# Another order and other engines for the small operations of a fused attention and two-layer kernel

## Chip, cores and metric

The kernel runs on one core of a Trainium2 chip. The metric is the device time of one execution in microseconds, as the median of several runs. All data starts in DRAM and the result ends there.

## What is computed

Chunked attention feeds two dense layers. The inputs q, k and v are 4 x 8 x 768 x 64 (batch, heads, sequence, head size), so there are 3072 tokens of 512 numbers.

```python
# attention: for every chunk of 32 queries, keys are 8 memory keys and the context from 16 left to 8 right
a = exp(s - max(s)); a = a / (sum(a) + 1e-9); out = a @ v_full
x = out.transpose(0, 2, 1, 3).reshape(3072, 512)
# first layer, w_in 512 x 1024, w_out 1024 x 512
h = x @ w_in
solu = h * softmax(h)
x = ((solu - mean(solu)) / sqrt(var(solu) + 1e-6) * g_ln) @ w_out
# second layer, w_in 512 x 2048, w_out 2048 x 512
h = x @ w_in
y = (h * clip(h + 3, 0, 6) / 6) @ w_out
```

The weights arrive as 64-bit floats and are turned into 32-bit ones on the chip.

## The kernel before, in words

**Tiles and precision.** Tokens are cut into 24 tiles of 128 (numbered 0 to 23). Every product with weights is done as three matmuls of type fp32r: each operand is split into a high part (on ACT, L337 and L895) and a low part, the difference (on VectorE or POOL, L341 and L898), and high x high, high x low and low x high are added up in PSUM.

**Weights.** A block of 128 x 512 is converted in steps: abs (L304 on ACT, L306 on VectorE), hold, a clamp (L311), three bit operations on VectorE (L315, L318, L321), then split or store. Names w1 and wo are those of the first layer, w2 those of the second. The 32 blocks of w2 are loaded, converted and written back to DRAM during the loop, two in a step; sum_pair (L848, L850 on POOL, four instructions) forms sums of blocks, and sums_out writes them, as the second layer uses a scheme of 7 products for blocks of 2 x 2.

**The order is written by hand.** Each engine runs its instructions in program order. The program is a list of names, expanded by a dispatcher; where an entry ends in a letter, P, D or A is the engine (POOL, VectorE, ACT). FIRST holds the fill, tiles 0 to 6 and, in entries that begin with @, step 7 of the loop. BODY is run for steps 8 to 23. LAST leads from the first layer to the second, a generator (unchanged) does the middle, CHANGE leads from the second layer's first product to its second, and a generated end (unchanged) closes.

**A step m of the loop** does, for tile m, m1 (x @ w_in in two halves of 12 matmuls, L694) and the ln_ entries: max (L703), exp (L709), den (L715), solu (L720), mean, sq, var, pow (L738 on POOL) and norm (L743). For a group of earlier tiles it does parts of m2 (@ w_out, L798), whose result m2_e copies out of PSUM as x2o (L808). For tile m - 1 it transposes solu (ln_p, L547 or L750) and splits it (ln_h L337, ln_l L341). For tiles ahead it runs attention: v_p (m + 1, L668), x_h and x_l (split of x, m + 1), s_max, s_sub, s_exp, s_sum and s_norm (softmax, m + 2; s_norm writes pn, L642), p_q (transposes of pn, m + 2, L583) with p_e (copies, L298), s_p (scores, m + 3, L540), and qk_p (transposes of q and k, m + 4, L547) with q_e and k_e (copies into kT, L298 on ACT, L300 on VectorE). qk uses the same PSUM buffer as m1's result h, so it waits until solu has read h, and the next m1 waits until q_e and k_e have read qk. k_e has four pieces: 0 is 128 x 448 and 1 is 128 x 256, pieces 2 and 3 are 128 x 96. DMAs are issued by SP, in program order too.

**The second layer.** mm(n) is one unit of 42 matmuls of 128 x 256 (L1006) into one of two sets of PSUM banks; o1 to o4 on VectorE (L1027, L1030, L1034, L1038) add up its products, then come relu (ACT, L1041) and clip (VectorE, L1044). Its operands are made by w_hi, w_lo, x_sum (POOL, L967), x_hi and x_lo. In the last stage, g4(i) is 21 matmuls (L1093) on operands from g_sum (L1072), g_hi and g_lo; g4:0 and g4:1 belong to one output tile, g4:2 to the next.

The conversion of w2 is tied to the step by these lines; a step handles block 2(m - 7) and block 2(m - 7) + 3:

```python
        def w2_of(m, x):
            u = 2 * (m - STEADY) + 3 * x
            return u if u < 2 * NF2 else None
```

Of the kernel before, what the change touches and what calls it, by code (L numbers as in the profile page):

```python
# [35 lines left out]
    w1_hi:0,P spread_mem_v:0,0,A s_rec:1 warm:4 v_p:0 s_norm:1,P p_p:1 k_e:3,1,A k_e:3,0,A w1_bits:4,1 s_max:2
    q_e:3,0,A q_e:3,1,A w1_bits:4,2 w1_hi:4,P load_k:4 s_sub:2 s_exp:2 w1_bits:5,2 load_q:4 x_h:0,0 s_p:3 s_sum:2
    k_p:4,0 x_l:0,0 p_e:1,1,A w1_hi:5,P warm:1 q_p:4 k_e:4,0,A w1_lo:4,D q_e:4,0,A p_e:1,0,A load_w1:2 w1_lo:5,D
    s_rec:2 load_v:1 s_max:3 w1_lo:0,P w1_abs:2,A load_q:5 spread_mem_v:1,0,A m1:0,0,0 load_w1:7 k_p:4,1
    spread_mem_v:1,64,A k_e:4,1,A s_norm:2,P w1_hold:2,D q_e:4,1,A w1_bits:2,0 w1_bits:2,1 m1:0,1,0 s_sub:3 s_exp:3  # L40
    v_p:1 load_w1:6 w1_bits:2,2 s_p:4 x_h:1,0 s_sum:3 x_l:1,0 load_k:5 w1_abs:7,A load_v:2 p_p:2 q_p:5 q_e:5,0,A
    s_rec:3 s_norm:3,D p_e:2,0,A w1_hi:2,P load_q:6 w1_lo:2,P w1_hold:7,D w1_abs:6,A w1_bits:7,0 w1_bits:7,1
    p_e:2,1,A q_e:5,1,A early_open m1:1,0,0 w1_bits:7,2 load_v:3 m1:1,1,0 w1_hold:6,D w1_bits:6,0 w1_bits:6,1
    w1_bits:6,2 w1_hi:7,A w1_lo:7,D m1:0,0,1 k_p:5,0 k_e:5,0,A load_k:6 w1_hi:6,A w1_lo:6,D load_wo:5 k_p:5,1 v_p:2
    k_e:5,1,A p_p:3 p_e:3,1,A load_wo:1 s_max:4 s_sub:4 p_e:3,0,A m1:0,1,1 ln_max:0 s_exp:4 m1:1,0,1 x_h:2,0 x_l:2,0
    k_p:6,1 s_p:5 ln_exp:0 s_sum:4 q_p:6 load_wo:0 m1:1,1,1 ln_den:0 k_p:6,0 q_e:6,1,A wo_abs:5,D wo_abs:1,A
    ln_solu:0 ln_mean:0 ln_sq:0 k_e:6,1,D ln_var:0 s_rec:4 wo_hold:5,D ln_max:1 s_norm:4,P load_wo:6 v_p:3 q_e:6,0,A
    m1:2,1,0 s_edge:5 s_max:5 s_sub:5 ln_exp:1 m1:2,1,1 m1:2,0,0 consts wo_abs:0,A ln_pow:0 load_wo:2 s_exp:5
    load_wo:7 k_mem:6,D k_e:6,0,A ln_den:1 p_p:4 x_h:3,1 wo_hold:1,P wo_bits:5,0 ln_norm:0 wo_bits:5,1 p_e:4,1,A
    s_sum:5 load_v:4 wo_bits:1,0 wo_hold:0,D ln_solu:1 wo_bits:5,2 x_l:3,1 ln_p:0,0 ln_h:0,0,1 m1:2,0,1 ln_p:0,1  # L50
    load_q:7 ln_mean:1 s_rec:5 ln_sq:1 ln_max:2 m1:3,1,0 ln_var:1 wo_bits:0,0 m1:3,1,1 load_wo:4 p_e:4,0,A load_k:7
    wo_bits:1,1 wo_abs:7,A wo_abs:6,A wo_bits:0,1 s_norm:5,D wo_hold:6,D wo_bits:0,2 s_p:6 ln_exp:2 wo_abs:4,D
    wo_bits:6,0 ln_den:2 ln_l:0,0,1 v_p:4 m1:3,0,0 load_g wo_hi:0 load_wo:3 ln_pow:1 x_h:4,1 wo_abs:2,D ln_h:0,1,1
    ln_solu:2 m1:3,0,1 ln_mean:2 ln_sq:2 x_l:4,1 wo_hold:4,D ln_norm:1 ln_p:1,0 ln_h:1,0,1 load_q:8 s_edge:6
    ln_max:3 s_max:6 wo_bits:6,1 wo_bits:1,2 s_sub:6 ln_p:1,1 ln_var:2 ln_pow:2 m1:4,1,0 p_p:5 ln_l:1,0,1 ln_exp:3
    p_e:5,1,A s_exp:6 wo_bits:4,0 q_p:7 ln_norm:2 p_e:5,0,A m1:4,1,1 m1:4,0,0 load_v:5 ln_l:0,1,1 q_e:7,1,A s_sum:6
    m1:4,0,1 wo_bits:6,2 q_e:7,0,A ln_p:2,0 ln_den:3 s_rec:6 wo_lo:0 wo_bits:4,1 k_p:7,0 ln_max:4 wo_hold:2,P
    k_e:7,0,D ln_h:1,1,1 ln_l:1,1,1 load_k:8 k_p:7,1 k_e:7,1,D early_close v_p:5 wo_abs:3,A ln_solu:3 ln_h:2,0,1
    ln_l:2,0,1 ln_p:2,1 ln_exp:4 ln_den:4 ln_solu:4 s_p:7 wo_hold:7,D k_p:8,0 x_h:5,1 s_norm:6,P p_p:6 wo_bits:2,0
    ln_h:2,1,1 p_e:6,0,A wo_bits:7,0 x_l:5,1 ln_l:2,1,1 k_e:8,0,A wo_hi:1 m1:5,1 p_e:6,1,D wo_bits:4,2 wo_hi:4  # L60
    k_p:8,1 load_v:6 wo_bits:2,1 v_p:6 wo_bits:2,2 ln_mean:4 ln_sq:4 wo_bits:7,1 ln_mean:3 wo_hold:3,P wo_lo:1
    wo_hi:2 q_p:8 wo_hi:5 wo_bits:3,0 wo_bits:3,1 m1:5,0 ln_sq:3 wo_lo:4 m2:0,0 wo_bits:3,2 wo_hi:3 wo_lo:2 wo_lo:5
    ln_var:3 load_v:8 wo_lo:3 m2:0,1 wo_hi:6 k_e:8,1,D wo_bits:7,2 x_h:6,1 s_max:7 ln_pow:3 wo_hi:7 x_l:6,1 m2:0,3
    load_w2:1 ln_norm:3 ln_max:5 ln_p:3,1 wo_lo:7 w2_abs:1,A wo_lo:6 ln_p:3,0 m2:0,4 m2:0,5 ln_exp:5 q_e:8,0,A
    ln_h:3,0,1 s_sub:7 q_e:8,1,A s_exp:7 ln_den:5 m2:0,2 ln_solu:5 ln_mean:5 m1:6,0 ln_l:3,0,1 m2_e:0,1 ln_sq:5
    ln_var:5 s_sum:7 s_rec:7 load_w2:0 w2_abs:0,A m2_e:0,0 m1:6,1 ln_var:4 ln_pow:5 ln_norm:5 ln_pow:4 w2_hold:1,D
    ln_h:3,1,0 s_norm:7,D p_p:7 w2_bits:1,0 load_k:9 ln_norm:4 load_v:7 ln_l:3,1,0 m2:0,6 ln_p:4,1 m2_s:0,0
    p_e:7,1,A ln_max:6 p_e:7,0,A ln_h:4,1,0 s_p:8 w2_bits:1,1 w2_bits:1,2 v_p:7 x_h:7,0 load_w2:3 load_k:10
    w2_store:1 ln_p:4,0 ln_l:4,1,0 ln_p:5,0 k_mem:9,D m2:0,7 w2_hold:0,D ln_exp:6 ln_den:6 ln_solu:6 ln_mean:6
    s_max:8 ln_sq:6 m2:0,8 ln_var:6 x_l:7,0 m2:0,9 m2:0,10 load_q:9 s_sub:8 s_exp:8 m2_e:0,2 ln_h:4,0,0 s_sum:8  # L70
    s_rec:8 s_norm:8,P ln_l:4,0,0 m2_s:0,1 m2:0,11 load_q:10 ln_h:5,0,0 q_p:9 load_v:9 q_go:9,A ln_l:5,0,0 m2_s:0,2
    block_p:9 ln_p:5,1 ln_h:5,1,0 load_k:11 block_e:9,A m2_e:0,3 w2_abs:3,A ln_pow:6 ln_norm:6 @m2:0 block_p:10
    block_e:10,A load_k:12 ln_l:5,1,0 late_turn p_p:8 w2_hold:3,P @qk_p_at:6 @k_e_at:6,3 @s_p_at:6 @k_e_at:6,0
    @s_max load_k:13 @q_e_at:6 @k_e_at:6,1 @k_e_at:6,2 load_q:11 @m2:2 m2_s:0,3 @s_sub @s_exp @w2_bits:0,0
    @w2_bits:0,1 @w2_bits:0,2 load_q:12 @w2_bits:1,0 @w2_bits:1,1 p_e:8,1,A p_e:8,0,A @w2_bits:1,2 @load_w2:0
    @w2_store:1 @sum_pair @sums_out @s_sum @s_norm @load_w2:1 @m1:0 @m1:1 @ln:max @w2_abs:0 @ln_p @ln:exp @ln:den
    @s_p @ln:solu @v_p @x_h @ln:mean @m2:3 @m2:1 @ln_h:0 @ln_l:0 @m2_e @qk_p @p_p @load_q @ln_h:1 @ln_l:1 @k_e:0
    @k_e:3 @x_l @q_e @k_e:1 @k_e:2 @load_k @k_mem @ln:sq @ln:var @w2_hold:0 @ln:pow @w2_abs:1 @p_e:1 @w2_hold:1
    @ln:norm @w2_store:0 @p_e:0 @m2_s @load_v
# [1410 lines left out]
```

## Time and profile before

| what | value |
|---|---|
| median of 3 runs | 869.97 us |
| lowest, highest | 866.45, 871.79 us |
| profiled execution | 870.14 us |
| its span | 868.3 us |
| TensorE matmul busy | 847.9 us, 98% of the span |
| VectorE (DVE) busy | 739.5 us, 85% |
| ScalarE (ACT) busy | 476.6 us, 55% |
| GpSimd (POOL) busy | 256.3 us, 30% |

PE is TensorE's matmul unit, DVE VectorE, ACT ScalarE, POOL GpSimd, SP the engine that issues DMAs. Times of the trace are counted from the start of the span; 1.84 us of the execution lie outside it. A busy time is an average over stages with different limits, so the windows of a stage are read beside it, and "idle before" an instruction, with the instruction that ended it, tells what an engine waited for.

### The profile page before, as it was taken

The numbers are of one execution on the slowest core, as the hardware profiler recorded it, in microseconds if no ns is written. First come the engines' busy times: TensorE is split into PE (matmuls) and PEld (weight loads), VectorE is DVE, ScalarE is ACT, GpSimd is POOL, SyncE is SP. The second block draws the span as 40 slices with busy tenths as digits, with TensorE's granted clock in tenths as the row PEclk, the third lists the DMA queues.
The fourth block names the chain that finished last, engine by engine and source line by source line (L and its number), as shares of the span: only waits on it lengthen the run. The fifth ranks groups of instructions, "written<-read, shape, count | busy, mean of one in ns | idle before, by whom it ended". The sixth has DMA issues, their size and how long they took to land.

```text
span 868.3 us, 21875 instructions
## 1 busy us (share of the span) xinstructions
PE 847.9 (98%) x8526; PEld 803.2 (92%) x8526; DVE 739.5 (85%) x1510; ACT 476.6 (55%) x946; POOL 256.3 (30%) x226
## 2 busy tenths in 40 slices
...
DVE  6899977787878779574999989889999999999995
...
GB/s 234 214 262 70 116 157 198 234 204 236 212 235 197 228 176 168 149 111 193 209 180 160 243 134 206 174 167 229 239 270 258 165 137 147 149 137 143 136 134 62
DMA packets 181552, 157.88 MB, mean 182 GB/s; under 512 B 105160, under 2 KB 155848, under 8 KB 181448
## 3 DMA queue, kind: packets, MB, share of 16 engines
...
q8 instruction: 67, 1.10, 0.5%
...
## 4 chain that ended last, share of the span: by engine, by line
PE 80%; DVE 11%; DMA 2%; issue 2%; ACT 2%; POOL 1%; DVEq 0%; POOLq 0%; ACTq 0%; SPq 0%
PE acc L1093 26%; PE acc L1006 21%; PE m L798 13%; PE h L694 10%; PE tp L668 2%; PE s L540 1%; DVE f_s L1044 1%; PE qk L547 1%; PE idle L1161 1%; PE tp L547 1%; DVE so L720 1%; PE sc L595 1%; DMA woraw<-in_moe_w_out_dram 1%; DVE lst L703 1%; PE tp L583 1%
## 5 line engine op out<-in xcount | busy, mean ns | idle before, releaser
L798 PE MATMUL m<-lnh,wo 128*128 128x256 f32 (+1 forms) x704 | 143.3, 295 | 3.7 <-DVE x2o L808 2.8
L798 PEld LDWEIGHTS m<-lnh,wo 128*128 128x128 f32 x704 | 113.9, 189 | 6.6 <-DVE x2o L808 3.1
L1041 ACT ACTIVATE f_s<-f_e,constants 128x512 f32<-128x512 f32 x96 | 67.9, 720 | 83.3 <-DVE f_e L1034 69.7
L694 PE MATMUL h<-w,xh 128*128 128x512 f32 x336 | 105.9, 396 | 1.1 <-ACT kT L298 1.1
L798 PE MATMUL m<-lnl,wo 128*128 128x256 f32 (+1 forms) x352 | 102.0, 290 | 0.0
L694 PEld LDWEIGHTS h<-w,xh 128*128 128x128 f32 x336 | 61.3, 188 | 13.0 <-ACT kT L298 1.3
L1044 DVE SCALAR_TENSOR_TENSOR f_s<-f_s,f_e 128x512 f32<-128x512 f32 x96 | 72.0, 758 | 0.7 <-ACT f_s L1041 0.7
L798 PEld LDWEIGHTS m<-lnl,wo 128*128 128x128 f32 x352 | 66.7, 189 | 0.6
L311 POOL TENSOR_SCALAR w2t<-w2t 128x512 f32<-128x512 f32 x30 | 59.8, 1992 | 20.8 <-ACT w2t L304 20.8
L694 PE MATMUL h<-w,xl 128*128 128x512 f32 x168 | 65.6, 390 | 0.0
L808 DVE COPY x2o<-m 128x512 f32<-128x512 f32 (+1 forms) x26 | 16.6, 646 | 40.8 <-PE m L798 39.6
L709 ACT ACTIVATE e<-h,lst 128x1024 f32<-128x1024 f32 x24 | 26.8, 1115 | 29.9 <-DVE lst L703 29.9
L895 ACT ACTIVATE b_qb<-f_kn 128x384 fp32r<-128x384 f32 (+1 forms) x48 | 27.7, 576 | 27.9 <-DVE f_kn L1072 15.4
L1030 DVE TENSOR_TENSOR f_e<-acc,f_e 128x512 f32<-128x512 f32 x48 | 32.9, 685 | 8.0 <-PE acc L1006 7.1
L694 PEld LDWEIGHTS h<-w,xl 128*128 128x128 f32 x168 | 31.5, 188 | 6.9
L642 POOL TENSOR_TENSOR pn<-pe,ast 128x512 f32<-128x512 f32 x21 | 22.3, 1063 | 50.5 <-DVE ast L638 40.3
L627 ACT ACTIVATE pe<-pe 128x512 f32<-128x512 f32 x24 | 15.2, 632 | 39.6 <-DVE pe L622 38.2
L703 DVE TENSOR_REDUCE lst<-h 128x1 f32<-128x1024 f32 x24 | 29.2, 1217 | 6.1 <-PE h L694 6.0
L1038 DVE TENSOR_TENSOR f_e<-acc,f_e 128x512 f32<-128x512 f32 x48 | 33.0, 687 | 1.1 <-PE acc L1006 0.2
L720 DVE SCALAR_TENSOR_TENSOR so<-h,lst,e 128x1024 f32<-128x1024 f32 x24 | 30.8, 1283 | 0.9
L341 DVE TENSOR_TENSOR lnl<-tp,lnh 128x512 fp32r<-128x512 f32 x41 | 28.1, 684 | 3.6 <-ACT lnh L337 3.6
L848 POOL TENSOR_TENSOR sums<-w2t,sums 128x256 f32<-128x256 f32 x24 | 20.8, 865 | 33.5 <-DVE w2t L321 33.5
...
## 6 DMA issues: line engine op xcount, KB each, us to landing
...
```

The costliest lines, as they stand in the source:

```text
L311: ENG[eng].tensor_scalar(out=tf, in0=tf, scalar1=U_LO, scalar2=U_HI, op0=ALU.max, op1=ALU.min)
L341: (POOL if far else DVE).tensor_tensor(lo, r, hi.bitcast(F32), ALU.subtract)
L694: PE.matmul(h[:, f], a[:, kt], w[kt][:, f * 512:(f + 1) * 512], start=n == 0, stop=n == 3 * NKT - 1)
L703: DVE.tensor_reduce(st_t[i][:, 2:3], h_t[i].rearrange("p a b -> p (a b)"), axis=AX.X, op=ALU.max, negate=True)
L720: DVE.scalar_tensor_tensor(out=so_t[i], in0=h_t.pop(i).rearrange("p a b -> p (a b)"), scalar=st[:, 5:6], in1=e_t[i], op0=ALU.mult, op1=ALU ...
L798: PE.matmul(acc, w[fc // 2][:, fc % 2, dc * P:(dc + 1) * P], a[:, fc], start=fresh and k == 0, stop=k == len(todo) - 1, skip_group_check=True)
L1006: PE.matmul(o, w[wl][:, c * P:(c + 1) * P], x[xl][:, c], start=m == 0 and half == 0, stop=m == 5, skip_group_check=True)
L1030: DVE.tensor_tensor(c_of(n)[1], bank(n % 2, 2), wide(c_of(n)[0][:, 1]), ALU.add)
L1038: DVE.tensor_tensor(c, bank(n % 2, 3), c, ALU.add)
L1041: ACT.activation(out=g_of(n)[k], in_=c_of(n)[k], func=AF.Relu, bias=three, scale=1.0)
L1044: DVE.scalar_tensor_tensor(out=g_of(n)[k], in0=g_of(n)[k], scalar=6.0, in1=c_of(n)[k], op0=ALU.min, op1=ALU.mult)
L1093: PE.matmul(bank(t % 2, k)[:, half], g[al][:, G_BLOCK[p]], b_op[j, p][bl], start=j == 0 and m == 0 and half == 0, stop=j == NU - 1 and m = ...
```

## The change

The set of operations is the same but for one form (ln_norm on ACT, two instructions, for tiles 4, 5 and step 7). What changes is the order of all four lists and the engine of some entries:

- w2: a step m handles block 2(m - 8) and block 2(m - 8) + 3, one step later than before; step 7 only converts block 1, and step 23 is the last with a block. sum_pair and sums_out follow.
- Engines in BODY: s_norm from POOL to VectorE, k_e 1, 2 and 3 from ACT to VectorE, w2_abs:0 from ACT to VectorE. Elsewhere: some conversions, copies and s_norm of the first list swapped between the three engines; the two block_e to VectorE.
- BODY's order, below in full. On TensorE only ln_p changes place, from behind qk_p to ahead of it. TURN, run in the last step, moves to near the start of the step.
- FIRST is rewritten as a whole.
- LAST: mm:0 moves from behind m2:10,7 to between m2:10,2 and m2:10,3; m2_e:9,1 comes ahead of m2_e:10,0.
- CHANGE: the order g4:0, g4:2, g4:1 becomes g4:0, g4:1, g4:2; the entries around them are shifted.

```diff
 BODY = """
-    m1:1 m1:0 w2_bits:0,0 m2:0 s_max w2_bits:0,1 w2_bits:1,0 s_sub w2_bits:0,2 ln:max w2_bits:1,1 s_exp w2_bits:1,2
-    sum_pair m2:1 ln:exp w2_store:0 v_p ln:den ln:solu s_sum s_p load_w2:0 x_h qk_p k_e:0 ln:mean q_e w2_store:1
-    k_e:1 w2_abs:0 k_e:3 s_norm k_mem w2_hold:0 ln_p m2:2 m2:3 load_w2:1 sums_out ln:sq load_v x_l turn m2_e k_e:2
-    p_p ln:var load_k ln_h:0 ln:pow ln_l:0 ln_h:1 ln:norm w2_abs:1 p_e:1 m2_s load_q ahead w2_hold:1 ln_l:1 p_e:0
+    s_max w2_bits:0,0 s_sub w2_bits:0,1 m1:1 turn w2_bits:0,2 m1:0 m2:0 m2:1 ln:max w2_bits:1,0 v_p w2_bits:1,1
+    ln:exp ln:den ln:solu w2_bits:1,2 s_exp sum_pair load_w2:0 ahead s_sum x_h w2_store:0 s_p ln_p ln:mean load_w2:1
+    ln:sq ln:var qk_p k_e:2,D x_l k_e:0,A k_e:3,D s_norm:D q_e:A k_e:1,D k_mem m2:2 m2:3 w2_abs:0,D sums_out ln_h:0
+    ln:pow m2_e:D ln_l:0 load_k ln_norm:D ln_h:1 w2_abs:1,A load_q p_p w2_hold:0,P m2_s w2_hold:1,P p_e:1,A ln_l:1
+    p_e:0,A load_v w2_store:1
 """
...
 LAST = """
...
-    load_w:5 load_w:4 w_lo:2 x_hi:0,2 x_hi:0,6 x_lo:0,2 w_hi:4 m2:10,2 m2_e:10,0 m2_e:9,1 x_sum:0,3 load_w:6 m2:10,3
-    m2_s:10,0 x_hi:0,4 m2:10,4 m2:10,5 x_lo:0,6 w_lo:4 w_hi:6 load_w:7 x_lo:0,5 m2_s:9,1 w_lo:6,pool w_hi:5 w_lo:5
-    load_w:8 w_hi:8 m2:10,6 m2:10,7 load_w:10 w_hi:7 m2_e:10,1 x_lo:0,4 mm:0 p1:0 o1:0 w_lo:7,pool load_w:9 m2:10,9
...
+    x_hi:0,2 ln_l:23,1 x_sum:0,4 x_hi:0,6 m2:10,0 m2:10,1 x_lo:0,2 x_sum:0,3 w_hi:4 w_hi:6 x_hi:0,4 m2:10,2 w_lo:3
+    load_w:7 w_hi:5 m2_e:9,1 w_hi:7 x_lo:0,4 x_lo:0,6 w_lo:6,pool load_w:10 w_hi:10 w_lo:4 m2_e:10,0 mm:0 p1:0
+    w_lo:5 m2:10,3 load_x:1 m2:10,6 w_lo:10,pool o1:0 m2:10,4 o2:0 m2:10,5 load_w:8 m2_s:9,1 load_w:14 m2:10,7 o3:0
...
 CHANGE = """
...
-    b_lo:13,1,pool g4:0 load_b:19 g_lo:2,0 g_hi:1,1 g_load:6 o3:47 g_lo:2,1 g_lo:1,1 relu:46,0 g_hi:4,0 relu:46,1
-    g_sum:4,1 g_sum:4,2 o4:47 g_lo:4,0 relu:47,0 fetch_b:21 clip:46,0 g_sum:3,1 relu:47,1 g_sum:4,4 b_hi:19,1
-    clip:46,1 g_sum:4,3 g_hi:4,1 g_sum:3,2 clip:47,0 g_lo:4,1 clip:47,1 fetch_b:22 g_sum:6,3 b_lo:18,1,pool g_sum:3,3
-    g_sum:3,4 g_sum:6,1 g4:2 g4:1 g_hi:3,0 g_hi:5,0 g_load:8 fetch_b:14 g_lo:3,0 g_load:7 g_sum:6,2 g_hi:3,1 g_hi:6,0
...
+    o2:47 g_hi:2,1 o3:47 g4:0 g_load:4 g4:1 g_store:44 g_lo:2,0 g_lo:2,1 relu:46,0 b_lo:13,1,pool clip:46,0
+    g_sum:4,1 g_load:3 fetch_b:14 o4:47 g_sum:3,1 g_store:45 g_sum:3,3 g_sum:3,2 relu:46,1 g_sum:4,2 g_sum:3,4
+    g_sum:4,3 g_sum:4,4 g_load:6 g_hi:4,0 fetch_b:22 fetch_b:15 g_lo:4,0 relu:47,1 g_hi:4,1 b_lo:18,1,pool clip:46,1
+    load_b:19 g4:2 g_lo:4,1 relu:47,0 g4:4 clip:47,0 clip:47,1 fetch_b:16 g_load:8 g_hi:6,0 g_sum:6,1 g_hi:5,0
...
-    def ln_norm(i):
+    def ln_norm(i, eng="D"):
         st = st_t.pop(i)
         so = so_t[i]
-        DVE.tensor_scalar(out=so, in0=so, scalar1=st[:, 7:8], scalar2=st[:, 10:11], op0=ALU.add, op1=ALU.mult)
+        if eng == "A":
+            ACT.activation(out=st[:, 11:12], in_=st[:, 7:8], func=AF.Copy, scale=st[:, 10:11])
+            ACT.activation(out=so, in_=so, func=AF.Identity, bias=st[:, 11:12], scale=st[:, 10:11])
+        else:
+            DVE.tensor_scalar(out=so, in0=so, scalar1=st[:, 7:8], scalar2=st[:, 10:11], op0=ALU.add, op1=ALU.mult)
...
         def w2_of(m, x):
-            u = 2 * (m - STEADY) + 3 * x
-            return u if u < 2 * NF2 else None
+            return 2 * (m - STEADY - 1) + 3 * x
+
+        def w2_next(m, x):
+            u = w2_of(m, x) + 2
+            return 0 <= u < 2 * NF2 and u != 1
...
-        def l_s_norm(m):
+        def l_s_norm(m, eng):
             if ok(m + 2):
-                s_norm(m + 2, "P")
+                s_norm(m + 2, eng)
 
         def pair_of(m):
-            return m % 2, (m - STEADY) // 2
+            return 1 - m % 2, (m - STEADY - 1) // 2
...
-        def l_k_e(m, n):
+        def l_k_e(m, n, eng):
             if ok(m + 4):
-                qk_k(m + 5, n, "A")
+                qk_k(m + 5, n, eng)
```

The other functions that take an engine now (l_p_e, l_q_e, l_w2_abs, l_w2_hold, l_m2_e) change in the same manner.

## Rows read from the trace of the kernel before

**Rows 1.** The page, parts 1 and 2: busy times, and VectorE in 40 slices.
```profile
PE 847.9 (98%) x8526; PEld 803.2 (92%) x8526; DVE 739.5 (85%) x1510; ACT 476.6 (55%) x946; POOL 256.3 (30%) x226
...
DVE  6899977787878779574999989889999999999995
```

**Rows 2.** What TensorE waited for: us in total, times, longest us.
```profile
PE m L798 <- DVE x2o L808: 2.8, 1, 2.8
PE tp L750 <- DVE sc L605: 1.4, 1, 1.4
...
PE h L694 <- DVE so L720: 1.1, 1, 1.1
PE h L694 <- ACT kT L298: 1.1, 1, 1.1
...
PE acc L1093 <- DVE f_e L1038: 1.0, 1, 1.0
...
PE tp L583 <- POOL pn L642: 0.5, 1, 0.5
```

**Rows 3.** Windows: us, then PE, PEld, DVE, ACT, POOL busy, PEclk, DMA, GB/s.
```profile
8.20:61.20 53.00, 51.80 (x550) 41.30 (x550) 46.37 (x85) 40.77 (x82) 20.17 (x20) 1.00 0.96 243
61.20:92.50 31.30, 28.94 (x280) 23.17 (x281) 31.04 (x51) 25.98 (x53) 16.13 (x13) 1.00 0.41 92
92.50:142.70 50.20, 47.13 (x515) 42.34 (x513) 38.09 (x66) 31.50 (x70) 14.52 (x14) 1.00 0.60 159
...
187.40:202.08 14.68, 14.68 (x206) 13.35 (x205) 11.67 (x21) 8.87 (x21) 8.62 (x9) 1.00 0.85 241
...
387.20:391.20 4.00, 3.99 (x14) 3.99 (x15) 3.41 (x4) 1.98 (x4) 1.59 (x2) 0.57 0.78 244
```

**Rows 4.** Timeline of a loop step, VectorE and TensorE: start us, us, engine, instruction.
```profile
193.47 1.21 DVE L703 TENSOR_REDUCE lst<-h 128x1 f32<-128x1024 f32 x1
...
197.80 0.46 PE L547 MATMUL qk<-ident,q_raw 64*128 64x64 f32 x8
...
201.77 0.60 PE L583 MATMUL tp<-ident,pn 128*128 128x128 f32 x4
...
203.90 0.69 DVE L341 TENSOR_TENSOR lnl<-tp,lnh 128x512 fp32r<-128x512 f32 x1
```

**Rows 5.** Groups by form: xcount, busy us, mean ns, idle before, releasers.
```profile
L642 DVE TENSOR_TENSOR pn<-pe,ast 128x512 f32<-128x512 f32 x3 | 2.2, 743 | 0.1
L642 POOL TENSOR_TENSOR pn<-pe,ast 128x512 f32<-128x512 f32 x21 | 22.3, 1063 | 50.5 <-DVE ast L638 40.3 <-DVE s L603 7.3 <-PE sc L595 2.8
L298 ACT ACTIVATE kT<-qk 128x96 f32<-128x96 f32 x27 | 7.1, 263 | 0.0
L300 DVE COPY kT<-kmT 128x128 f32<-128x128 f32 x7 | 1.5, 218 | 0.2
L306 DVE TENSOR_SCALAR wot<-woraw 128x512 uint32<-128x512 uint32 x2 | 0.8, 413 | 0.0
L304 ACT ACTIVATE w2t<-w2raw 128x512 f32<-128x512 f32 x32 | 21.4, 669 | 6.7 <-DMA w2raw<-in_moe_w_in_dram 3.7 <-issue 3.0
L298 ACT ACTIVATE kT<-qk 128x256 f32<-128x256 f32 x13 | 5.0, 388 | 0.0
```

**Rows 6.** Timeline, SP's queue and ACT: one load of w2 and its first use.
```profile
314.26 0.38 SPq L429 DMA_DIRECT2D w2raw<-in_moe_w_out_dram  x1
...
322.99 0.68 ACT L304 ACTIVATE w2t<-w2raw 128x512 f32<-128x512 f32 x1 [2.99 <-issue]
```

**Rows 7.** Timeline of the transition to the second layer: POOL, VectorE and TensorE.
```profile
380.88 1.75 POOL L967 TENSOR_TENSOR f_pn<-f_v,f_pe 128x512 f32<-128x512 f32 x1
381.41 1.78 DVE L898 TENSOR_TENSOR b_wb<-f_pb,b_wb 128x512 fp32r<-128x512 f32 x1
...
384.81 0.68 DVE L898 TENSOR_TENSOR b_wb<-f_qb,b_wb 128x512 fp32r<-128x512 f32 x1
...
386.02 1.14 DVE L808 COPY x2o<-m 128x384 f32<-128x384 f32 x2
...
387.21 0.45 PE L798 MATMUL m<-lnh,wo 128*128 128x384 f32 x1 [2.80 <-DVE x2o L808]
```

More of the change, by code (lines that the diff above doesn't have):

```diff
@@ L36 @@
[L36 to L79, printed above, removed]
+    zero:km0,D zero:km1,D zero:kn0,D load_w1:1 w1_abs:1,A idle_fill:10 idle_fill:19 load_mem_k:0 load_q:0 mem_p:0
@@ new lines @@
+    ln_h:0,0,1 load_v:5 wo_abs:7,A ln_l:0,0,1 wo_bits:0,0 wo_bits:0,1 wo_bits:1,1 load_k:8 ln_max:2 wo_bits:0,2
+    s_p:6 wo_abs:4,A wo_hold:4,D ln_norm:1,D ln_exp:2 ln_den:2 wo_abs:6,D wo_bits:4,0 ln_p:0,1 x_h:4,1 wo_hi:0
+    s_edge:6 wo_bits:1,2 ln_p:1,0 ln_h:0,1,1 m1:3,1,0 m1:3,1,1 ln_solu:2 wo_hold:6,D x_l:4,1 m1:4,0,0 ln_mean:2
+    ln_sq:2 ln_var:2 q_p:7 ln_p:1,1 wo_bits:6,0 wo_bits:6,1 ln_pow:2 s_norm:5,D s_max:6 ln_h:1,0,1 ln_norm:2,D
+    s_sub:6 q_e:7,0,A q_e:7,1,A ln_l:1,0,1 p_p:5 s_exp:6 ln_max:3 ln_l:0,1,1 p_e:5,1,A m1:4,0,1 p_e:5,0,A s_sum:6
```

203 lines of the change are left out of this document (122 added, 81 removed).

## Prediction

> **What bounds the kernel now.** I read the page first: busy times, then the slices. TensorE's matmul engine is busy in 98% of the span, VectorE in 85%, and VectorE's slices reach 9 in several stretches [rows 1]. So TensorE is the bound nearly everywhere, and the order and engine of small operations can only buy back what it idles, or make it idle more. Its waits come next. The ones that matter are few and named [rows 2]: 2.8 us for x2o, the output copy of the first layer; 1.4 and 1.1 us in the front for VectorE; 1.1 us for ACT's copies to kT; 1.0 us for the third output addition, just before the last stage's products go on; 0.5 us for POOL's pn. All the waits of that view together make 14.4 us, those left out here under 1 us each but for 2.3 at the start, with 1.7 us more where the clock was down (below). That is the purse.
>
> Then the windows [rows 3]. From 8.20 to 61.20 us TensorE was busy 51.80 of 53.00 us, part of it with filler matmuls. From 61.20 to 92.50 it lost 31.30 - 28.94 = 2.36 us while VectorE was busy 31.04 of 31.30: there VectorE is the bound. From 92.50 to 142.70 it lost 50.20 - 47.13 = 3.07 us. One step of the loop lasts 14.68 us, all of them TensorE's, with VectorE at 11.67, ACT at 8.87 and POOL at 8.62 us. There the change cannot win, only lose. Last, the timeline of a step and of the transition.
>
> The profiled execution took 870.14 us (span 868.3 and 1.84 around it), 0.17 above the median shown. I subtract from 870.1.
>
> **The loop, 16 steps.** The list of operations is the same, so TensorE's 14.68 stay. Three edits load VectorE. s_norm leaves POOL, 1063 ns, for VectorE, 743 ns. Three of four k_e copies leave ACT; VectorE's nearest copies take 218 ns (128x128), and the 96-column ones 263 on ACT. The abs of one weight block costs 413 ns on VectorE against 669 on ACT [rows 5]. I take 0.74 + 2 x 0.2 + 0.4 (the 256-column copy, 388 on ACT) + 0.41 = 1.95; not all steps have all, and over the loop I count 26.7 us, or 1.67 a step. VectorE comes to 11.67 + 1.67 = 13.3 us of 14.68. It holds, with 1.3 to spare. Below, the bound is nothing gained or lost; above, the first rival.
>
> In-order queues ask for more than a sum. In the step shown, which begins at 187.40, the maximum starts at 193.47 (6.07 into it), and qk, which waits for solu's read of the shared bank, at 197.80 (10.40) [rows 4]. The new order puts five short VectorE entries (0.4 to 0.7 each, 2.7 in all at their spacing) ahead of the maximum, and the last ln_l of the step before ends 2.5 us into the step (203.90 + 0.69 - 202.08 [rows 4]). That gives 5.2 to 5.9: no later than now. solu then ends near 9.9, half a microsecond before it is needed. s_norm, behind x_l and two k_e copies, ends at 13.3 to 13.9; its transpose is due at 201.77 - 187.40 = 14.37 [rows 4]. Slack 0.4 to 1: I take 0. One wait goes: p_q:22 waited 0.5 for POOL [rows 2], where s_norm was behind the long clamps of POOL's queue; on VectorE nothing long is before it. Gain 0.55.
>
> **Weights one step later.** Three bit instructions of the first x = 0 block, about 2.0 us of VectorE, leave step 7, which lies in the loaded front, and turn up in step 23, which had none. In step 23 they are covered by 14.68 of TensorE. In the front they are part of the next term.
>
> **The front.** Ahead of the last wo_lo that the first m2 needs, VectorE's list sums to 85.7 us before and 86.1 after, pricing each entry by its form: no shorter. What can shrink is its idle time before 61 us (53.00 - 46.37 = 6.6 [rows 3]) and the order in which results fall due. ln_norm:3 and wo_lo:6 come 1.4 and 3.2 us earlier in the list, and the whole first list falls from 110.5 to 107.4. Up to 99 us TensorE waits 4.9 in all, 1.4 and 1.1 of it in rows 2. I take 1.5 back; the ends are +4.9 and, as a rearranged saturated queue may be late elsewhere, -1.5.
>
> From 99 us to the loop, 0.54 + 1.10 + 0.62 = 2.3 us are lost, the 1.1 for kT on ACT [rows 2]. The k_e copies now lie earlier or on VectorE, and step 7's VectorE list is 10.1 instead of 12.0. Late x_h and x_l of tile 8 cost about 0.8 by my count. Gain 1.4 (0 to 2.3).
>
> **LAST.** mm:0, the first product of the second layer, moves from behind m2:10,7 to between m2:10,2 and m2:10,3. Before, m2:10,3 began at 387.21 after 2.80 idle, since m2_e:9,1 had to empty its bank, and on VectorE's queue that copy (386.02, two together 1.14) stood behind two 1.78 us splits [rows 7]. After the pause the granted clock was 0.57 over 4.00 us, that is near the lower of its two levels (1.2 of 2.4 GHz), against 1.00 in the stages shown [rows 3]: 4.00 x 0.43 = 1.7 lost too. mm:0 is 42 matmuls of about 115 ns, 4.9 us. It covers the 2.8 and keeps TensorE busy, so the 1.7 goes as well, if its operands are there. x_lo:0,4 is the late one: by POOL's sums I put it at 385 to 386, and mm:0 reads it at about 387. Gain 4.5; less 1.0 for what VectorE, full in the stretch that follows, gives back (0 to 1.5, or all 4.5 if the operand is late). I take 3.5.
>
> **CHANGE.** g4:1 now follows g4:0 and goes on in the same output tile's PSUM, so the 1.0 us wait for the third addition [rows 2] is filled by 21 matmuls. VectorE is full here; I take 0.5 (0 to 1.0). The code after the last matmul isn't touched.
>
> Sum: 0.55 + 1.5 + 1.4 + 3.5 + 0.5 = 7.4. 870.1 - 7.4 = 862.7 us.
>
> **A rule that speaks against it.** A POOL addition of 1.75 us started at 380.88, and VectorE's split at 381.41 took 1.78 instead of the 0.68 of its like at 384.81 [rows 7]. The Trainium skill, "Perfetto Trace Analysis", section "Optimizing Scalar/DVE Operations", says that the two engines share a read port and that shifting work between them may not help; the trace agrees for splits, which took 2.6 times as long, and no row shows s_norm on VectorE beside POOL's pair sums. The mechanism here, from rows, is the third rival.
>
> **Rivals.**
> First, slower: w2_abs:0 on VectorE holds the whole queue until its DMA has landed. On ACT the same wait cost nothing. One block was asked for at 314.26 and converted at 322.99, after 2.99 idle [rows 6], 8.7 us later; the new order has about 8.5 us between issue and use. For it: behind the abs stand m2_e, ln_norm, both ln_l and the next maximum. Against it: of 32 blocks only 6.7 us of idle was before the conversion [rows 5]. It decides once the wait exceeds the 1.3 us to spare: 2.99 - 1.35 = 1.6 a step, 13 us if half the steps have it, 862.7 + 13.1 = 875.8; in ten steps or more it passes 878.7.
> Second, no gain where VectorE is full: the front keeps its 4.9 and the transition gives the 3.5 back, as VectorE's sum past 392 us doesn't change. What stays is 0.55 and about 0.8: 868.7.
> Third, POOL's four pair sums (0.7 to 1.0 each) now run beside s_norm. If it waits for one, it ends at 14.0 to 14.6 against 14.37: 0.25 a step, 4.0 in all, 866.7.
> Fourth, the front loses its waits wholly, because VectorE's early idle time is used: 3.4 more, and the give-back of 1.0 and the 0.8 don't come: 862.7 - 5.2 = 857.5.
>
> **How the numbers follow.** Forecast 0.45 (its own range 858 to 868), first rival 0.12, second 0.15, third 0.08, fourth 0.20. About 1% is what a measurement of this kernel tells from no change: 861.3 and 878.7. Faster is the fourth and two fifths of the forecast, 0.20 + 0.18 = 0.38. Slower is two thirds of the first, 0.08. Same is the rest, 0.54. The range 854 to 876 leaves out the dearer half of the first rival and the fastest part of the fourth, with unknown mishaps under 0.2.
>
> **What would show it.** Right: the loop's step at 14.68 with VectorE at 13 to 13.5; no wait for x2o near 387 and clock 1.00 there; under 3.5 us of waits from 61 to 99; no pn wait. Wrong: a step of 15 or more, with VectorE's rows after w2_abs late (first rival) or s_norm over 1 us long (third); mm:0 waiting for x_lo; new waits for o1 to o4 between 400 and 460.

## The result and the profile after

The changed kernel took 856.07 us (median of 4 runs, 855.08 to 857.3), the kernel before 868.49 us in the same comparison: a ratio of 0.985 with an interval of 0.982 to 0.989. It is faster by 12.4 us where 7.4 were forecast, inside the stated range of 854 to 876 and below the 858 to 868 of the forecast itself.

The page of the changed kernel, its busy times and VectorE (DVE) in slices:

```profile
PE 845.4 (99%) x8526; PEld 802.0 (94%) x8526; DVE 760.9 (89%) x1578; ACT 464.5 (54%) x893; POOL 253.2 (30%) x214
...
DVE  6999867999999999776999988998999999999995
```

Against [rows 1], VectorE has 21 us more to do and TensorE's share rises by one per cent of a shorter span. The view of TensorE's waits is nearly empty; it answers to [rows 2] (engine, tile and line, waited for; us in total, times, longest):

```profile
PE idle L1162 <- POOL ident masks.py:199: 1.3, 1, 1.3
PE m L804 <- DVE x2o L814: 0.6, 1, 0.6
PE acc L1099 <- DVE f_e L1040: 0.6, 1, 0.6
...
PE h L696 <- DVE kT L302: 0.3, 1, 0.3
```

All waits of the front that rows 2 show (sc, so, kT) are gone or down to 0.3, pn is gone, x2o fell from 2.8 to 0.6. The 0.6 for f_e at L1040 is a wait for o3; the 1.0 of before, at L1038, was one for o4. Windows of the changed kernel (columns as in [rows 3]), in this order: the front as in [rows 3], the whole part up to tile 6's m1, a loop step, and the product that was moved (mm:0).

```profile
61.20:92.50 31.30, 31.06 (x299) 25.86 (x298) 30.52 (x55) 29.41 (x60) 18.11 (x14) 1.00 0.68 155
...
0.00:99.03 99.03, 96.46 (x918) 79.92 (x919) 86.84 (x161) 75.96 (x151) 45.93 (x45) 1.00 0.80 198
...
180.46:195.14 14.68, 14.68 (x208) 13.35 (x206) 13.84 (x26) 9.17 (x19) 8.52 (x8) 1.00 0.85 232
...
376.40:381.40 5.00, 5.00 (x45) 5.00 (x44) 4.07 (x6) 1.79 (x3) 1.50 (x2) 1.00 0.50 143
```

In the front TensorE now loses 0.24 us of 31.30 (before 2.36) although VectorE is still busy 30.52 us. The step keeps its 14.68 us with VectorE at 13.84. Where mm:0 now stands the clock is 1.00.

A ledger follows from the starts of the same work in both timelines (us; the last column is what the stage gave). In the last stage the products are counted by their matmuls, 21 to a g4:

| start of | before | after | gained so far | stage |
|---|---|---|---|---|
| m1 of tile 3 | 61.19 | 60.71 | 0.5 | fill: 0.5 |
| m1 of tile 6 | 103.94 | 99.03 | 4.9 | front: 4.4 |
| m1 of tile 9 | 158.03 | 151.10 | 6.9 | to the loop: 2.0 |
| m1 of tile 23 | 361.61 | 353.81 | 7.8 | loop: 0.9 |
| mm(2) | 410.98 | 399.46 | 11.5 | transition: 3.7 |
| mm(12) | 460.78 | 447.06 | 13.7 | ten products on: 2.2 |
| 17th g4 | 672.09 | 659.80 | 12.3 | CHANGE: -1.4 |
| end of the last matmul | 862.75 | 850.47 | 12.3 | the rest: 0 |

So three questions were left: why the front, the three rows up to tile 9's m1, gave 6.9 and not 2.9, what in LAST (the transition and the ten products behind it) gave 5.9 and not 3.5, and why CHANGE cost 1.4 instead of giving 0.5.

### The profile page after: what moved, and what is told of

Its sections match the earlier page's. It is cut to its first block, busy times and chain, and to the rows that moved or that the text cites. A ratio compares the mean times of both kernels' runs of the same rounds, so it can differ in the third digit from the quotient of the medians.

```text
span 855.5 us, 21813 instructions
## 1 busy us (share of the span) xinstructions
PE 845.4 (99%) x8526; PEld 802.0 (94%) x8526; DVE 760.9 (89%) x1578; ACT 464.5 (54%) x893; POOL 253.2 (30%) x214
## 4 chain that ended last, share of the span: by engine, by line
PE 85%; DVE 7%; DMA 3%; SPq 2%; ACT 2%; issue 1%; POOL 0%; DVEq 0%; POOLq 0%; ACTq 0%
PE acc L1099 25%; PE acc L1012 23%; PE m L804 15%; PE h L696 12%; PE tp L670 2%; PE s L542 1%; PE tp L549 1%; DVE f_s L1050 1%; PE qk L549 1%; DMA woraw<-in_moe_w_out_dram 1%; SPq L399 1%; PE idle L1162 1%; PE tp L585 1%; DMA f_xo<-sums 1%; DMA w1raw<-in_moe_w_in_dram 1%
## 5 line engine op out<-in xcount | busy, mean ns | idle before, releaser
L313 POOL TENSOR_SCALAR w2t<-w2t 128x512 f32<-128x512 f32 x31 | 66.7, 2161 | 16.6 <-DVE w2t L308 15.5
L901 ACT ACTIVATE b_qb<-f_kn 128x384 fp32r<-128x384 f32 (+1 forms) x48 | 27.6, 575 | 23.2 <-DVE f_kn L1078 12.1
L740 POOL TENSOR_TENSOR lst<-lst,constants 128x1 f32<-128x1 f32 x24 | 17.3, 722 | 58.8 <-ACT lst L736 58.8
L300 ACT ACTIVATE pb<-tp 64x512 f32<-64x512 f32 x46 | 27.2, 592 | 6.1 <-PE tp L652 4.3
L904 DVE TENSOR_TENSOR b_pb<-f_kn,b_qb 128x384 fp32r<-128x384 f32 (+1 forms) x48 | 29.5, 616 | 0.0
```

The costliest lines, as they stand in the source:

```text
L313: ENG[eng].tensor_scalar(out=tf, in0=tf, scalar1=U_LO, scalar2=U_HI, op0=ALU.max, op1=ALU.min)
L904: eng.tensor_tensor(hl[1], r, hl[0].bitcast(F32), ALU.subtract)
```

## Experiments

Every kernel below is the changed one with one thing put back or moved. The kernel before was measured again beside each group of them, with medians of 868.2 to 869.7 us, so medians of different groups that lie 1.5 us apart may be the same.

**The old first list.** FIRST of before, with the entries for the x = 0 block of step 7 taken out:

```diff
 FIRST = """
-    zero:km0,D zero:km1,D zero:kn0,D load_w1:1 w1_abs:1,A idle_fill:10 idle_fill:19 load_mem_k:0 load_q:0 mem_p:0
...
+    zero:v1,P zero:kn1,D zero:km1,D zero:v0,D load_q:0 idle_fill:10 q_p:0 load_w1:1 zero:kn0,P zero:qb,P q_e:0,0,A
...
```

> The changed kernel with the first list of before in its order and on its engines, the second weights still one step later (the entries for the x = 0 block taken out of that list). Theory A, the new first list is what takes the waits from 61 to 154 us away: TensorE starts m1 of tile 9 at 156 to 158 us as before (158.0) and not at 151.1, total 861 to 863 us. Rival B, the later weights did it, since they take 2 us and more off the loaded VectorE: start at 151 to 153, total 856 to 858.

It took 863.57 us, ratio 0.992 (0.990 to 0.995), and tile 9's m1 began at 157.06. The waits are back, as the view of TensorE's waits of this kernel shows:

```profile
PE tp L755 <- DVE sc L606: 1.6, 1, 1.6
...
PE h L695 <- ACT kT L299: 1.1, 1, 1.1
PE h L695 <- DVE so L721: 0.9, 1, 0.9
PE m L803 <- DVE wo L420: 0.9, 2, 0.5
```

Theory A holds in its start of 156 to 158 us, and its total came out 0.6 above the range: the first list is worth 6.0 us up to tile 9's m1 and 7.5 by the medians. The later weights by themselves gave at most the 1.0 us between 158.03 and 157.06.

**The new order with the old engines.** In the new first list, 42 entries go back to the engine of before, such as:

```diff
-w1_abs:1,A
+w1_abs:1,D
...
-q_e:1,0,A
+q_e:1,0,D
...
-k_e:8,1,A
+k_e:8,1,D
```

> The changed kernel with its new order in the first list, but 42 of the 43 entries that changed their engine back on the engine of before. Theory A1, the order does it (VectorE is kept busy earlier and the late results fall due in time): m1 of tile 9 within 1.5 us of 151.1, total 856 to 858 us. Rival A2, the engines do it (VectorE relieved of clamps and copies in the front): m1 of tile 9 at 155 us or later, total 860 us or more.

It took 876.22 us, ratio 1.007 (1.004 to 1.009), 0.7% slower than before. By the numbers A1 is out, but A2's reason is not shown either: 8.6 of the 20 us arise before tile 0's m1 (40.25 instead of 31.62), where VectorE is busy 23.2 of 40.25 us. Later, one copy, k_e:8,1 on VectorE behind the wo conversions, costs one wait, a row of this kernel's waits of TensorE:

```profile
PE tp L754 <- DVE kT L300: 3.6, 1, 3.6
```

So a third theory, C, was put up: order and engine only work together. Two kernels tell it from A2. One puts back only the 15 entries ahead of tile 0's m1:

> The changed kernel, with only the 15 entries ahead of tile 0's m1 on the engine that they had before (zeroing, conversion of the first weights w1, a few copies and s_norm:0). Theory C, order and engine belong together: in the new order these engines make queues that wait for a DMA or for each other, as in the run with 42 entries put back; TensorE starts m1 of tile 0 at 38 to 41 us instead of 31.6 and the delay is kept, total 863 to 866 us. Rival: the early delay gives VectorE, which is full from 60 us on, time to work ahead, so most of it is won back by tile 9: total under 860 us.

It took 864.47 us, ratio 0.995 (0.993 to 0.997); tile 0's m1 began at 41.14 and tile 9's at 158.94, so 7.8 of the 9.5 us of delay were kept. Where it begins is seen in VectorE's timeline of this kernel:

```profile
12.90 0.68 DVE L300 COPY qb<-tp 64x512 f32<-64x512 f32 x1 [4.19 <-ACT w1raw L304]
13.51 0.41 DVE L315 TENSOR_SCALAR w1raw<-w1raw 128x512 uint32<-128x512 uint32 x1
```

q_e:1,0, now on VectorE, waits 4.19 us, and the first weight's bits stand behind it: 13.51, where the changed kernel has them at 8.31. TensorE then waits for ACT and VectorE in its fill:

```profile
PE sc L595 <- ACT kT L298: 2.6, 2, 2.1
PE tp L490 <- DVE kmT L300: 1.4, 1, 1.4
```

The granted clock is lower there too, as the window of 20.00 to 31.60 shows, first of this kernel, then of the changed one:

```profile
20.00:31.60 11.60, 9.61 (x63) 7.22 (x62) 6.51 (x14) 5.25 (x11) 5.02 (x7) 0.55 0.73 169
```

```profile
20.00:31.60 11.60, 11.45 (x149) 9.19 (x150) 11.20 (x22) 9.92 (x20) 5.75 (x7) 1.00 0.80 184
```

The other kernel keeps the old order and takes all new engines:

> The changed kernel with the first list in the order of before, but all its entries on the engines of after (weights one step later, as in the run with the old first list, which took 863.6 us). Rival A2, the engines by themselves relieve VectorE: total 860 us or less, fewer waits for VectorE from 61 to 99 us. Theory C, order and engine belong together: no gain against 863.6, total 863 us or more, with new waits where the old order has the entry late on the new engine.

It took 867.46 us, ratio 0.999 (0.997 to 1.000): the engines alone are worth nothing here, they cost 3.9 us against the old list, with new or longer waits of TensorE:

```profile
PE tp L756 <- DVE sc L607: 2.3, 1, 2.3
PE h L696 <- ACT kT L300: 2.2, 1, 2.2
```

Of its delay, 4.5 us arise before tile 0's m1 (35.66 instead of the old list's 31.16). So both of these totals hang much on the fill. The stretch from tile 3's m1 to tile 6's lies behind it, and there theory C can be read without the fill. "Slowed" are VectorE's instructions that took over 0.15 us more than their form's quick price (a tenth of its instructions in all fourteen traces are as quick or quicker), with what they took above it in sum:

| first list | stretch, us | VectorE busy, us | slowed |
|---|---|---|---|
| kernel before | 42.8 | 41.8 | 7, by 5.0 us |
| old order, old engines | 42.9 | 41.9 | 7, by 5.0 us |
| old order, new engines | 42.2 | 41.3 | 5, by 4.2 us |
| new order, 42 old engines | 45.1 | 40.6 | 3, by 3.2 us |
| new order, 15 old engines | 37.9 | 36.7 | 3, by 1.0 us |
| changed kernel | 38.3 | 37.0 | 3, by 1.0 us |

VectorE runs 66 or 67 instructions in each of the six, and the 45.1 has the wait of 3.6 for kT in it. Neither half of the change does it here either, and the 15 early engines have no part in this stretch. Theory C holds at both ends.

**The loop's engines and its list.**

```diff
-    ln:sq ln:var qk_p k_e:2,D x_l k_e:0,A k_e:3,D s_norm:D q_e:A k_e:1,D k_mem m2:2 m2:3 w2_abs:0,D sums_out ln_h:0
+    ln:sq ln:var qk_p k_e:2,A x_l k_e:0,A k_e:3,A s_norm:P q_e:A k_e:1,A k_mem m2:2 m2:3 w2_abs:0,A sums_out ln_h:0
```

> The changed kernel with the three loaded edits of the loop undone: s_norm on POOL, k_e 1 to 3 and w2_abs:0 on ACT, same order. Theory: the loop's step is TensorE's 14.68 us with either engine, VectorE only falls from 13.8 to about 12 us a step; total 855.5 to 857.5, with at most one wait for pn of 0.5 us or so back. Rival: the moves are what lets the step run without waits, since ACT's copies hold up the next m1; then 0.2 us a step or more come back, 859 us or more.

It took 856.36 us, ratio 0.984 (0.981 to 0.988), no different from the changed kernel. The same step of it as the changed kernel's above, by its window:

```profile
178.18:192.86 14.68, 14.68 (x208) 13.36 (x206) 12.14 (x21) 9.55 (x22) 9.90 (x9) 1.00 0.84 225
```

VectorE has 1.7 us less in it, and TensorE's 14.68 stand. No wait for pn came back, though s_norm is on POOL again. With the whole BODY of before instead:

> The changed kernel with the loop's list of before, order and engines, weights one step later. Theory: the loop is bound by TensorE in both lists, so the step stays 14.68 us; what returns is the one wait for pn (0.5) and the waits at the seam between the first list and the loop, since the lists were laid out for each other: 856.5 to 859 us. Rival: the new list of the loop carries part of the front's gain: 860 us or more, with waits in step 8.

It took 859.2 us, ratio 0.988 (0.985 to 0.992). Its longest new waits of TensorE are one at qk in step 8, the seam (146.08), and one for a norm behind the loop (369.28):

```profile
PE qk L549 <- issue: 1.2, 1, 1.2
...
PE tp L756 <- DVE so L749: 0.7, 1, 0.7
```

The theory holds for the seam, its upper end a little low, but its wait for pn did not return: s_norm was on POOL in the old order too, and the view has no row for pn. The steps between are bound by TensorE, though not alike: with the old list every other one lasts about 14.75 us, in this kernel as in the kernel before, and TensorE is busy in all of it. One such step of the kernel before:

```profile
202.13:216.88 14.75, 14.74 (x207) 13.37 (x206) 11.70 (x21) 8.86 (x21) 9.40 (x9) 1.00 0.80 208
```

With the new order nearly all steps have 14.68, on either engines. What TensorE spends the 0.07 on stays open.

**LAST.** mm:0 and its first readers go back behind m2:10,7, in the new list:

```diff
-    load_w:7 w_hi:5 m2_e:9,1 w_hi:7 x_lo:0,4 x_lo:0,6 w_lo:6,pool load_w:10 w_hi:10 w_lo:4 m2_e:10,0 mm:0 p1:0
-    w_lo:5 m2:10,3 load_x:1 m2:10,6 w_lo:10,pool o1:0 m2:10,4 o2:0 m2:10,5 load_w:8 m2_s:9,1 load_w:14 m2:10,7 o3:0
+    load_w:7 w_hi:5 m2_e:9,1 w_hi:7 x_lo:0,4 x_lo:0,6 w_lo:6,pool load_w:10 w_hi:10 w_lo:4 m2_e:10,0
+    w_lo:5 m2:10,3 load_x:1 m2:10,6 w_lo:10,pool m2:10,4 m2:10,5 load_w:8 m2_s:9,1 load_w:14 m2:10,7 mm:0 p1:0 o1:0 o2:0 o3:0
```

> The changed kernel with mm:0 and what reads it (p1:0, o1:0, o2:0) back behind m2:10,7; the rest of the new list for the transition stays. Theory D1, mm:0 is the cover that keeps TensorE busy while x2o is copied: a wait of 2 us or more for x2o comes back at m2:10,3, with a lower clock behind it, total 859 to 861 us. Rival D2, what helped is that VectorE's copy m2_e:9,1 is earlier in its queue: m2:10,3 waits 1 us or less, the clock stays, total 856 to 858 us.

It took 864.35 us, ratio 0.996 (0.994 to 0.997), 8 us more than the changed kernel and so beyond D1's 859 to 861. Its waits of TensorE have one row for x2o:

```profile
PE m L803 <- DVE x2o L813: 6.0, 2, 3.5
```

The first of the two waits is 3.5, and the granted clock from 376 to 380 is 0.74. D2 is out: the copies stand no later in VectorE's queue than in the changed kernel, and without the cover they are waited for. m2_e:9,1 was done at 375.22 and m2:10,3 still began only at 378.03, just behind the other copy, m2_e:10,0, which ended at 377.97. The second wait, 2.4 at 393.97, is for a copy that stands behind o1 to o4 in both lists; here o1 had to wait for the later mm:0 (388.93 instead of 382.72). So not all 8 us are the cover's.

The whole LAST of before:

> The changed kernel with the list LAST of before. By the ledger of the two traces the new list gave 3.7 us up to mm(2) and 2.2 us in the ten products behind it. Theory: all of it goes, total 861 to 862.5 us, with the wait of 2 to 3 us for x2o at m2:10,3 and a low clock behind it. Rival, the 2.2 us come from TensorE's arriving 8 us earlier and not from the list: total 859 to 860.5 us.

It took 862.57 us, ratio 0.992 (0.989 to 0.995): just above the theory's range. The 2.2 us behind the transition go too: the ten products take 50.9 us (49.8 before, 47.6 in the changed kernel), with a wait of 1.8 us for a POOL split there:

```profile
PE m L803 <- DVE x2o L813: 2.8, 1, 2.8
PE acc L1011 <- POOL b_wo L903: 1.8, 1, 1.8
```

And the old LAST with mm:0 alone ahead of m2:10,3, the splits that it needs with it:

```diff
-    m2:10,3
...
-    x_lo:0,4 mm:0 p1:0
...
+    x_hi:0,4 w_lo:4 w_hi:6 x_lo:0,6 x_lo:0,5 w_lo:6,pool x_lo:0,4 mm:0 p1:0
+    m2:10,3
```

> The list LAST of before with one edit: mm:0, and the splits of its operands that stood behind m2:10,3, go ahead of m2:10,3. Theory D1, the cover alone does most of it: against the run with the old list 3 us or more are won up to mm(2), no wait over 1 us for x2o. Rival D3, the splits of VectorE were the limit, so mm:0 waits for x_lo or w_lo instead, 2 us or more: against the old list 1.5 us or less are won.

It took 864.32 us, ratio 0.995 (0.993 to 0.997): nothing won, D3. The profiled execution took 870.01, 5.7 above this median, so its trace tells what waits for what, and its sizes are not those of the median. The wait for x2o is down to 0.7, as D1 has it. But mm:0 itself waits, for the low part of x that the prediction had in time, a row of its waits:

```profile
PE acc L1011 <- DVE b_z L903: 2.5, 1, 2.5
```

The split began late and took 1.75 us, beside a POOL split; both from the timeline of this kernel:

```profile
382.60 1.51 POOL L903 TENSOR_TENSOR b_wb<-f_qb,b_wb 128x512 fp32r<-128x512 f32 x1 [1.46 <-ACT b_wb L900]
```

```profile
382.91 1.75 DVE L903 TENSOR_TENSOR b_z<-f_pn,b_z 128x512 fp32r<-128x512 f32 x1
```

So the gain in LAST is neither the cover alone nor the new queue alone: the cover removes one wait, and only the new queue has the cover's own operands ready.

**CHANGE.** With the list of before:

> The changed kernel with the list CHANGE of before. From mm(44) to the fourth g4 the changed kernel took 1.4 us more than before. Theory E1, the new list does it (o3 behind other VectorE work, operands of g4 late): that stretch falls by 1 to 1.8 us, total 854.3 to 855.3 us. Rival E2, VectorE is full here whatever the order, and TensorE comes 13 us earlier to the same work: the stretch stays within 0.4 us, total 855.7 to 856.5 us.

It took 854.65 us, ratio 0.985 (0.982 to 0.987). What the expectations call the fourth g4 is the start of the fourth 42 matmuls of the last stage, which is the seventh g4 of 21. The stretch from mm(44) up to it fell from 36.2 to 35.1 us, and the total lies in E1's range too. But its interval overlaps the changed kernel's, and kernels with the new list had this stretch at 33.4 to 36.7, so E1 is not shown. What differs between them shows in the timeline of the changed kernel, VectorE's clips first, then POOL's splits beside them:

```profile
602.34 1.50 DVE L1050 SCALAR_TENSOR_TENSOR f_s<-f_s,f_e 128x512 f32<-128x512 f32 x1
604.37 0.67 DVE L1050 SCALAR_TENSOR_TENSOR f_s<-f_s,f_e 128x512 f32<-128x512 f32 x1
...
608.02 1.64 DVE L1050 SCALAR_TENSOR_TENSOR f_s<-f_s,f_e 128x512 f32<-128x512 f32 x1
```

```profile
602.00 1.29 POOL L904 TENSOR_TENSOR b_lh<-f_xo,b_lh 128x512 fp32r<-128x512 f32 x1
607.82 1.29 POOL L904 TENSOR_TENSOR b_ll<-f_xo,b_ll 128x512 fp32r<-128x512 f32 x1 [4.53 <-ACT b_ll L901]
```

The two slow clips start beside one of POOL's low parts, and each ends 0.55 us after it does (603.29 and 609.11); alone, a clip takes 0.67. So a clip's price there is what is left of POOL's instruction, and 0.55 more. This was put up as F2, against the order of the three g4:

```diff
-    o2:47 g_hi:2,1 o3:47 g4:0 g_load:4 g4:1 g_store:44 g_lo:2,0 g_lo:2,1 relu:46,0 b_lo:13,1,pool clip:46,0
+    o2:47 g_hi:2,1 o3:47 g4:0 g_load:4 g_store:44 g_lo:2,0 g_lo:2,1 relu:46,0 b_lo:13,1,pool clip:46,0
...
-    load_b:19 g4:2 g_lo:4,1 relu:47,0 g4:4 clip:47,0 clip:47,1 fetch_b:16 g_load:8 g_hi:6,0 g_sum:6,1 g_hi:5,0
+    load_b:19 g4:2 g4:1 g_lo:4,1 relu:47,0 g4:4 clip:47,0 clip:47,1 fetch_b:16 g_load:8 g_hi:6,0 g_sum:6,1 g_hi:5,0
```

> The changed kernel with g4:1 back behind g4:2, the rest of the new list CHANGE kept. Theory F1, the order of the three g4 is worth the wait for o4:47 that it covers: g4:2 waits 0.3 to 1.0 us for it, total 0.3 to 1.0 us above the changed kernel's 856.1. Rival F2, what sets this stretch is VectorE, slowed where its clips (two inputs in SBUF) start beside POOL's low parts, 1.5 us instead of 0.7: from mm(43) to the fourth g4 the time goes with the number of VectorE instructions over 0.9 us (one: 38.8 us, two: 39.8, four: 40.6 to 41.9 in the traces so far), whatever the order; total within 0.5.

It took 856.08 us, ratio 0.985 (0.982 to 0.988). The wait that F1 names did come, one row of this kernel's waits of TensorE:

```profile
PE acc L1098 <- DVE f_e L1043: 0.7, 1, 0.7
```

But the stretch is no longer for it, so this order of the g4 is worth nothing that could be measured. From mm(43) to the seventh g4, with the number of VectorE instructions over 0.9 us in it:

| kernel (list CHANGE) | us | slowed |
|---|---|---|
| old LAST (new) | 38.2 | 1 |
| old order, new engines in FIRST (new) | 38.8 | 1 |
| last kernel below (old, g4:1 moved) | 39.3 | 1 |
| before (old) | 39.6 | 1 |
| 15 old engines in FIRST (new) | 39.8 | 2 |
| old CHANGE (old) | 39.9 | 2 |
| old FIRST (new) | 40.0 | 2 |
| 42 old engines in FIRST (new) | 40.1 | 3 |
| old BODY (new) | 40.6 | 4 |
| old LAST with mm:0 moved (new) | 40.6 | 4 |
| g4:1 behind g4:2 (new) | 41.1 | 5 |
| mm:0 late (new) | 41.3 | 4 |
| changed kernel (new) | 41.4 | 4 |
| old loop engines (new) | 41.9 | 4 |

One list has any time from 38.2 to 41.9, and it goes with the slowed instructions. Each of these, in all fourteen traces, ran beside a POOL split and ended 0.55 us after it, or 0.15 where it is one of 128 x 128: they are collisions of the two engines. That the collisions set the time of the stretch was not tested by an edit: no kernel took POOL's splits out of it, and why they fall differently in kernels with the same list stays open.

Last, the old CHANGE with g4:1 ahead of g4:2, as a version that might beat both:

```diff
-    g_sum:3,4 g_sum:6,1 g4:2 g4:1 g_hi:3,0 g_hi:5,0 g_load:8 fetch_b:14 g_lo:3,0 g_load:7 g_sum:6,2 g_hi:3,1 g_hi:6,0
+    g_sum:3,4 g_sum:6,1 g4:1 g4:2 g_hi:3,0 g_hi:5,0 g_load:8 fetch_b:14 g_lo:3,0 g_load:7 g_sum:6,2 g_hi:3,1 g_hi:6,0
```

> The changed kernel with the list CHANGE of before, in which g4:1 goes ahead of g4:2. The run with the old CHANGE took 854.65 us and had two slowed VectorE instructions in the stretch and a wait of 0.99 us for o4:47. Theory F1: that wait is filled, 853.7 to 854.4 us. Theory F2: nothing or little, 854.4 to 855.2 us, as VectorE is full and the operands of g4:1 come no earlier.

It took 856.29 us, ratio 0.985 (0.982 to 0.988): no better than the changed kernel. The wait for o4:47 is gone, and a new one of 1.1 for a DMA has come, in this kernel's waits of TensorE:

```profile
PE acc L1098 <- DMA b_xah<-b_d: 1.1, 1, 1.1
```

No version tried beats the changed kernel beyond the interval.

## Why the prediction was right in sign and short in size

**The loop.** Right. The step stayed at 14.68 us, VectorE came to 13.84 (13.3 forecast), s_norm cost 718 ns on VectorE and pn is waited for no more. The first rival did not come: the abs on VectorE holds nobody up, and taken back to ACT it changes nothing. The loop gave 0.9 (0.55 forecast), but the reason given is not shown: with s_norm on POOL, in the new order or the old, no wait for pn came back. Of the 0.9, 0.3 are fewer waits (0.55 before, 0.2 after), and the rest is time in which TensorE is busy, a part of it the 0.07 that every other step of the old list takes longer.

**The third rival** cost next to nothing. In the loop's step at 180.46 POOL's pair sums lie from 186.1 to 189.7, and s_norm starts at 193.13. In the next step they end at 208.2, s_norm starts beside the last one at 208.0, and it takes 0.78 us instead of 0.68; the longest in the loop took 0.96. What the prediction did not weigh is the same meeting of the two engines in CHANGE and in the front, where it cost most (a clip of 0.67 us takes 1.5 and 1.64 above).

The Trainium skill, "Perfetto Trace Analysis", section "Optimizing Scalar/DVE Operations", says that the two engines share a read port and that moving work between them might not help. The runs agree: s_norm is 0.3 us cheaper on VectorE, and the kernel with it back on POOL is as fast (856.36).

**The front: the step that failed** is "VectorE's list sums to 85.7 us before and 86.1 after, pricing each entry by its form: no shorter". The list is no shorter in entries, but its sum by mean prices is wrong. The window up to tile 6's m1 shows VectorE busy 86.84 us with 161 instructions (above), where before it was, by the same view of the kernel before:

```profile
0.00:103.94 103.94, 96.59 (x919) 78.90 (x920) 91.40 (x156) 78.02 (x155) 42.27 (x44) 1.00 0.74 185
```

That is 4.6 us less for five instructions more, and TensorE gets there 4.9 us earlier. Mean prices hid it: the same form costs more where it meets POOL. In the groups of VectorE between 60 and 104 us, before:

```profile
L315 DVE TENSOR_SCALAR woraw<-woraw 128x512 uint32<-128x512 uint32 x5 | 3.5, 718 | 0.0
L311 DVE TENSOR_SCALAR woraw<-woraw 128x512 f32<-128x512 f32 x2 | 1.5, 765 | 0.0
L311 DVE TENSOR_SCALAR wot<-wot 128x512 f32<-128x512 f32 x1 | 1.4, 1367 | 0.0
L743 DVE TENSOR_SCALAR so<-so,lst 128x1024 f32<-128x1024 f32 x3 | 3.8, 1258 | 0.0
```

and the same view of the changed kernel:

```profile
L317 DVE TENSOR_SCALAR woraw<-woraw 128x512 uint32<-128x512 uint32 x6 | 2.7, 457 | 0.3 <-POOL woraw L313 0.2
L313 DVE TENSOR_SCALAR woraw<-woraw 128x512 f32<-128x512 f32 x3 | 1.3, 419 | 0.0
L313 DVE TENSOR_SCALAR wot<-wot 128x512 f32<-128x512 f32 x1 | 0.4, 415 | 0.0
L749 DVE TENSOR_SCALAR so<-so,lst 128x1024 f32<-128x1024 f32 x3 | 2.4, 803 | 0.0
```

The clamp of 1367 ns (wot at L311) began beside a POOL split; free of POOL it takes 415. Both lines are from the timeline of the kernel before:

```profile
68.37 1.37 DVE L311 TENSOR_SCALAR wot<-wot 128x512 f32<-128x512 f32 x1
```

```profile
68.17 1.29 POOL L341 TENSOR_TENSOR xl<-far,xh 128x512 fp32r<-128x512 f32 x1 [4.69 <-ACT xh L337]
```

The table of the first lists above has the sum: from tile 3's m1 to tile 6's the slowed instructions cost 5.0 us before and 1.0 after, which is 4.0 of the 4.4 us that this stretch gave. That link is read from rows; no kernel changed the collisions alone.

The term of 1.5 (up to 99 us) measured 4.9, and the term of 1.4 (from there to the loop) 2.0. The fourth rival, which I had at 0.20, comes nearest (857.5), but its reason, VectorE's early idle time, is not what the runs show: that idle time fell from 6.6 to 4.4 us (8.20 to 61.20), and tile 3's m1 began only 0.5 us earlier. Even the 0.5 is no gain that can be told from chance, as nine kernels with the same first list reached tile 3's m1 between 58.8 and 62.8.

**LAST.** Against the gain of 4.5 the transition gave 3.7, with the cover that was forecast, but the operand's time was right by luck. The prediction put x_lo:0,4 at 385 to 386 and its reading at about 387; with the old splits it was late, and mm:0 waited 2.5 us for it. It was in time because the new list brings the splits forward, so that mm:0 ran from 376.45 without a wait. The 1.0 that VectorE was to give back had the wrong sign: the ten products behind gave 2.2 more. Together 5.9 where 3.5 were forecast.

**CHANGE.** The gain of 0.5 did not come. The wait of 1.0, which is one for the fourth addition (o4, L1038) and not for the third, is filled, and a new one of 0.6 for o3 came. The order of the g4 is worth nothing; VectorE is busy 39.9 of 41.4 us from mm(43) to the seventh g4. The 1.4 us lost go with the collisions, four in the changed kernel's profile and one in that of before; that they are the cause is argued, not tested.

Together 12.3 = 6.9 + 0.9 + 3.7 + 2.2 - 1.4. Put back one at a time, the four lists cost 7.5, 3.1, 6.5 and -1.4 us by the medians, 15.7 in sum: the lists were laid out for each other, as the wait at the seam shows, and their gains don't simply add.
